# Decode attention kernel: TensorE's whole step sequence and most of VectorE's put into hardware loops

## The chip, the cores and the metric

One core of one Trainium2 chip runs the kernel. The metric is device microseconds of one execution (lower is better). Every number quoted as a time is a median over the kernel's runs; no slow run enters a comparison.

All instants below count from the span's start, that is, from the first instruction of the profiled execution. In the views of the profile PE is TensorE (PEld its weight loads), DVE is VectorE, ACT is ScalarE, POOL is GpSimd, and SPq is the queue of SyncE that issues the loads.

## The reference, cut to what matters

```python
B, Sq, D = 4, 1, 512
H, Sk, Dh = 32, 8192, 128
k_cache, v_cache: (B, H, Sk, Dh) bf16        # 268 MB each

q = (x_norm @ wq) -> (B, H, 1, Dh)
scores = einsum("bhqd,bhkd->bhqk", q, k_cache) * Dh ** -0.5
p = softmax(scores)
o = einsum("bhqk,bhkd->bhqd", p, v_cache)
h = x + o @ wo
out = h + glu(layernorm(h))                  # w_gate, w_up: 512x1792, w_down: 1792x512
```

One query per head against 8192 keys: 551 MB must be read, and every byte of K and V is used for one query row. Reading is the work.

## The kernel before

K and V are loaded in 64 tiles each (4 MB: two heads), K and V alternating, into a ring of four slots. A "step" is one head: VectorE transposes its K (four instructions of 1.2 us), TensorE makes the scores, and ten steps later TensorE multiplies the probabilities with V (PV). Eight steps make a group, whose softmax runs as a chain of small operations over all engines.

```python
GS = 8
LAG = 10
NS = 4
L0, LB = 16, 16          # steps 16..127 of TensorE are a loop of 7 turns of 16 steps

class _Prog:
    ...
    def emit(self, name, e):
        seen = {}
        turns = self.turns(name) if name == "pe" else []
        for op in self.ops[name]:
            if name == "pe" and op.turn is not None:
                if op is turns[0][0]:
                    self.emit_loop(name, e, turns, seen)
                continue
            ...                                  # any other operation: written out
```

```python
        # ring slots go round: wq, k0..k4, then k and v in turn
        for it in items:
            ...
            slot_of[it] = cur
            prev_of[it] = [owner[cur]] if owner[cur] is not None else []
            owner[cur] = it
            cur = (cur + 1) % NS
        ...
        def dve_T(s):
            it = ("k", s // 2)
            src, buf, base = slot_of[it], s % 2, (s % 2) * HT
            q = HT // 4
            op = None
            for i in range(4):
                def f(e, i=i):
                    return e.transpose(kT[:, buf, i * q:(i + 1) * q].bitcast(U32),
                                       ringv(src)[:, base + i * q:base + (i + 1) * q].bitcast(U32))
                op = P("dve", f, [dma_of[it][0], sc_of.get(s - 2)])
                yield
            T_of[s] = op
            consumed[it] = op
        ...
        for s in range(NST + LAG + 4):
            prog.turn = (s - L0) // LB if L0 <= s < NST else None
            ...                                  # the step's operations, with the groups' chains
```

A load of slot X waits until the tile that was in X has been consumed. Each engine's operations share one semaphore, so in the loop every turn must hold the same operations; small "blank" operations stood in for groups that do not exist yet. VectorE (661 instructions of work), ScalarE and the queue that issues the loads are written out in full.

## Time and profile before

| | before |
|---|---|
| time, median (6 runs) | 1289.76 us (1289.60 to 1290.04) |
| profiled span | 1288.0 us |
| data read | 550.77 MB at 428 GB/s |
| busy: TensorE, VectorE, ScalarE | 39%, 50%, 6% |

From the page of the kernel before: engines' busy time with share of the span, then two rows of 40 time slices (busy tenths of the DMA engines, GB/s), then the DMA queues (packets, MB, share of the 16 engines' span).

```profile
span 1288.0 us, 11045 instructions
PE 496.7 (39%) x4851; PEld 187.4 (15%) x4851; DVE 638.2 (50%) x661; ACT 77.3 (6%) x151; POOL 8.1 (1%) x23
...
DMA  9999999999999999999999999999999999999997
GB/s 407 431 430 431 431 430 432 429 432 428 436 431 431 431 432 433 430 434 430 434 429 435 430 433 429 434 429 435 428 436 427 436 427 436 428 435 429 434 429 311
...
q1 hardware_dynamic: 20384, 550.78, 99.5%
q8 instruction: 12, 0.20, 0.1%
q14 instruction: 7, 0.06, 0.0%
...
DMA 85%; PE 12%; DVE 2%; issue 0%; SPq 0%; DVEq 0%
```

What to read: the DMA engines are busy 90% or more in every slice but the last (70 to 80%), and the chain of work that ended last (the last line, by engine) is 85% DMA. No compute engine is full (50% at most). q8 and q14 are not data. The page calls their kind instruction and counts their packets, 12 and 7, on the same 16 DMA engines. They are 0.26 MB of 551 MB, 0.05%.

From the groups and the issue list of the kernel before (a group's last part is idle time of the engine before these instructions and what ended it; an issue's last number is us from issue to landing):

```profile
L457 DVE STREAM_TRANSPOSE kT<-ring 128x1024 uint32<-128x1024 uint32 x512 | 588.4, 1209 | 478.3 <-DMA ring<-in_A_k_cache_dram 478.3
...
ring<-in_A_k_cache_dram SPq DMA_DIRECT2D x64, 4096.0 KB, 29.7
ring<-in_A_v_cache_dram SPq DMA_DIRECT2D x64, 4096.0 KB, 33.8
...
kT<-in_A_wo_dram SPq DMA_DIRECT2D x1, 2560.0 KB, 40.4
```

VectorE waits 478 us for K tiles, so VectorE is not what holds the loads. A tile takes 9.71 us to stream, and 30 to 34 us pass from issue to landing, so two other tiles are queued ahead of each new one.

From the chain of work that ended last of the kernel before, two places (start us, us, what): each shown line is the first PV of every second V tile, so of every fourth tile in all, at the moment that tile had landed.

```profile
451.94 1.90 PE PS L504 x16
...
490.79 1.90 PE PS L504 x16
...
530.62 1.90 PE PS L504 x16
...
569.49 1.90 PE PS L504 x15
...
724.95 1.90 PE PS L504 x16
...
764.77 1.90 PE PS L504 x16
...
803.62 1.90 PE PS L504 x16
```

Four tiles take 38.85 us (490.79 - 451.94), as they should at 9.71 each. But 490.79 to 530.62 is 39.83, and 724.95 to 764.77 is 39.82: about once in 235 us the stream loses one microsecond.

The trace also records when each of a load's 16 increments of its semaphore arrives: every K and V tile shows 16 separate instants. I read each as one of the 16 DMA engines that the page counts, ending its share of the tile; the records do not name the engine. The work waits for the last of the 16: where TensorE had been idle for over 1 us before a PV (63 times), the PV started 0.04 us (median; 0.14 at most) after the last increment of a tile. I call the time from the first to the last of them the *lag* of the latest DMA engine. Worked out from these records (not a view of the profile), around one of the long intervals:

```
kernel before    last of 16 at   since last of tile before   first of 16, since first of tile before   lag
                 510.18 us         9.72                        9.73                                     2.30
                 520.86 us        10.68                        9.70                                     3.28
                 530.58 us         9.72                        9.71                                     3.29
```

The fastest DMA engine keeps its pace. One engine loses 0.98 us and does not get it back, and because the work on a tile starts after the last of its 16 increments, the whole kernel is 0.98 us later from there on. An 8 KB packet of q14 starts at 510.9 us.

### The profile page before, as it was taken

What the parts mean: (1) busy time and instruction counts of PE and PEld (TensorE: products, weight loads), DVE (VectorE), ACT (ScalarE), POOL (GpSimd) and SP (SyncE); (2) the same over time, 40 slices, a digit from 0 to 9 for tenths busy, and PEclk for the clock granted to TensorE, in tenths of its full rate; (3) what the DMA queues carried; (4) which work ended last, traced back from release to release, by engine and by line L of the source; (5) the groups of instructions that cost most, each with busy time, mean ns of one, the idle gap of its engine ahead of it and who ended that gap; (6) DMA issues with size and microseconds to landing.
All of it is one profiled execution on the core that took longest, in us unless ns stands there. A gap on an engine that the chain in (4) does not pass through costs nothing.

```text
span 1288.0 us, 11045 instructions
## 1 busy us (share of the span) xinstructions
PE 496.7 (39%) x4851; PEld 187.4 (15%) x4851; DVE 638.2 (50%) x661; ACT 77.3 (6%) x151; POOL 8.1 (1%) x23
## 2 busy tenths in 40 slices
PE   3434334335244244333334343252342442343445
PEld 1011111111011011111111111020110111111114
DVE  5974644535545545535536445455445446355300
ACT  2010100001010010100101000010100101000011
POOL 2000000000000000000000000000000000000000
PEclk9995565565665565665665665655655656655665
DMA  9999999999999999999999999999999999999997
GB/s 407 431 430 431 431 430 432 429 432 428 436 431 431 431 432 433 430 434 430 434 429 435 430 433 429 434 429 435 428 436 427 436 427 436 428 435 429 434 429 311
DMA packets 20411, 551.04 MB, mean 428 GB/s; under 512 B 2212, under 2 KB 2216, under 8 KB 3624
## 3 DMA queue, kind: packets, MB, share of 16 engines
q1 hardware_dynamic: 20384, 550.78, 99.5%
q8 instruction: 12, 0.20, 0.1%
q14 instruction: 7, 0.06, 0.0%
q10 hardware_dynamic: 8, 0.00, 0.0%
HBM read 550.77 MB, written 0.00 MB: 428 GB/s over the span
## 4 chain that ended last, share of the span: by engine, by line
DMA 85%; PE 12%; DVE 2%; issue 0%; SPq 0%; DVEq 0%
DMA ring<-in_A_v_cache_dram 79%; PE PS L504 7%; PE PS L482 4%; DMA ring<-in_B_w_up_dram 3%; DMA ring<-in_A_k_cache_dram 2%; DVE kT L457 1%; DMA ring<-in_A_wq_dram 1%; PE PS L535 0%; PE PS L387 0%; PE PS L720 0%; DVE Lq L430 0%; DVE ring L404 0%; PE PS L414 0%; PE PS L734 0%; DVE mx L518 0%
## 5 line engine op out<-in xcount | busy, mean ns | idle before, releaser
L457 DVE STREAM_TRANSPOSE kT<-ring 128x1024 uint32<-128x1024 uint32 x512 | 588.4, 1209 | 478.3 <-DMA ring<-in_A_k_cache_dram 478.3
L482 PE MATMUL PS<-kT,Lqg 128*32 128x512 bf16 x2048 | 241.7, 619 | 566.8 <-DVE kT L457 560.3
L504 PE MATMUL PS<-ring,PTz 128*32 128x512 bf16 x2048 | 215.1, 565 | 200.1 <-DMA ring<-in_A_v_cache_dram 200.1
L482 PEld LDWEIGHTS PS<-kT,Lqg 128*32 128x32 bf16 x2048 | 69.6, 135 | 697.2 <-DVE kT L457 449.4
L504 PEld LDWEIGHTS PS<-ring,PTz 128*32 128x32 bf16 x2048 | 65.8, 128 | 317.6 <-DMA ring<-in_A_v_cache_dram 190.1
L565 DVE STREAM_TRANSPOSE Et<-Ep 128x512 bf16<-128x512 bf16 x16 | 11.4, 711 | 96.3 <-ACT Ep L561 96.3
L539 ACT ACTIVATE negm<-PS 128x1 f32<-128x1 f32 x16 | 2.7, 171 | 672.3 <-PE PS L535 672.3
L574 ACT ACTIVATE PTz<-Et 64x512 bf16<-64x512 bf16 x32 | 34.0, 1061 | 12.8 <-DVE Et L565 12.5
L602 ACT ACTIVATE A_sb<-PS 32x32 bf16<-32x32 f32 x16 | 3.7, 231 | 480.3 <-PE PS L600 480.3
L579 DVE TENSOR_SCALAR Zs<-PS,rinv 128x512 f32<-128x512 f32 x16 | 11.6, 723 | 27.1 <-PE PS L504 27.1
L586 PE MATMUL PS<-SelZ,Zs 128*128 128x8 f32 x128 | 17.7, 265 | 0.9 <-DVE Zs L579 0.9
L586 PEld LDWEIGHTS PS<-SelZ,Zs 128*128 128x128 f32 x128 | 16.3, 199 | 10.2 <-issue 8.8
L518 DVE TENSOR_REDUCE mx<-PS 128x1 f32<-128x512 f32 x16 | 10.5, 657 | 4.3 <-PE PS L482 4.2
L541 ACT ACTIVATE E_sb<-PS,negm 128x512 bf16<-128x512 f32 x16 | 11.0, 687 | 0.5
L561 ACT ACTIVATE Ep<-PS 128x512 bf16<-128x512 f32 x16 | 9.6, 597 | 10.1 <-PE PS L557 10.1
L546 PEld LDWEIGHTS PS<-sig,Gsum 128*128 128x128 f32 x32 | 7.8, 304 | 13.1 <-issue 13.1
L546 PE MATMUL PS<-sig,Gsum 128*128 128x1 f32 x32 | 9.2, 356 | 0.0
L535 PEld LDWEIGHTS PS<-onesf,rowx 1*128 1x128 f32 x32 | 6.8, 262 | 12.3 <-issue 12.3
L535 PE MATMUL PS<-onesf,rowx 1*128 1x1 f32 x32 | 8.1, 321 | 0.0
L720 PE MATMUL PS<-hnT,ring 128*128 128x4 bf16 x112 | 7.0, 199 | 2.9 <-DMA ring<-in_B_w_gate_dram 2.1
L720 PEld LDWEIGHTS PS<-hnT,ring 128*128 128x128 bf16 x112 | 6.9, 161 | 3.1 <-DVE hnT L711 2.2
L557 PE MATMUL PS<-E_sb,Sel 128*32 128x512 bf16 x64 | 6.5, 400 | 1.9 <-ACT E_sb L541 1.1
(89 smaller groups left out, 93.2 us busy)
## 6 DMA issues: line engine op xcount, KB each, us to landing
ring<-in_A_k_cache_dram SPq DMA_DIRECT2D x64, 4096.0 KB, 29.7
ring<-in_A_v_cache_dram SPq DMA_DIRECT2D x64, 4096.0 KB, 33.8
ring<-in_A_wq_dram SPq DMA_DIRECT2D x1, 4096.0 KB, 12.3
kT<-in_A_wo_dram SPq DMA_DIRECT2D x1, 2560.0 KB, 40.4
ring<-in_B_w_gate_dram SPq DMA_DIRECT2D x1, 1792.0 KB, 39.7
ring<-in_B_w_up_dram SPq DMA_DIRECT2D x1, 1792.0 KB, 43.7
kT<-in_A_wo_dram SPq DMA_DIRECT2D x1, 1536.0 KB, 43.5
ring<-in_B_w_down_dram SPq DMA_DIRECT2D x1, 896.0 KB, 36.6
```

The lines of the kernel that those rows point to most:

```text
L457: return e.transpose(kT[:, buf, i * q:(i + 1) * q].bitcast(U32), ringv(src)[:, base + i * q:base + (i + 1) * q].bitcast(U32))
L482: mm = e.matmul(bS[g % 2][32 * j:32 * (j + 1), :], Lqg[:, g % 2, l0:l0 + 32], rhs, start=(s % GS == 0 and v == 0), stop=(s % GS == GS - 1 ...
L504: mm = e.matmul(bO[g % 2][32 * rq:32 * (rq + 1), :], PTz[:, g % 2, l0:l0 + 32], ringv(slot)[:, r0 * 128:(r0 + 4) * 128], start=(s % GS == ...
L518: mx_of[g] = P("dve", lambda e: e.tensor_reduce(mx[:, :], bS[g % 2][:, :], AX.X, ALU.max), [sc_of[g * GS + GS - 1], p1_of.get(g - 1)])
L535: p2_of[g] = P("pe", lambda e: e.matmul(bX[:, 0:1], rowx[0:1, :], onesf[0:1, 0:1], start=True, stop=True), [d2b_of[g], c_ones])
L541: exp_of[g] = P("act", lambda e: e.activation(E_sb[:, :], bS[g % 2][:, :], ACT.Exp, bias=negm[:, 0:1], scale=SCALE, accum_out=sig[:, 0:1]) ...
L546: L_of[g] = P("pe", lambda e: e.matmul(bX[:, 0:1], Gsum[:, :], sig[:, 0:1], start=True, stop=True), [exp_of[g], a1_of[g], d_g])
L565: et_of[g] = P("dve", lambda e: e.transpose(Et[:, :], Ep[:, :]), [epc_of[g]] + list(ptc_of.get(g - 1, ())))
L574: return e.activation(dst, src, ACT.Copy)
L579: z_of[g] = P("dve", lambda e: e.tensor_scalar(Zs[:, :], bO[g % 2][:, :], rinv[:, g % 2:g % 2 + 1], None, op0=ALU.mult), [pv_of[g * GS + G ...
L586: mm = e.matmul(bP[1][:, 0:8], Zs[:, 128 * r:128 * (r + 1)], SelZ[:, r, :], start=(r == 0), stop=(r == 3))
L720: mm = e.matmul(bk[:, B * t:B * t + B], wv[:, c, t:F:NFT], hnT[:, B * c:B * c + B], start=(c == 0), stop=(c == NDC - 1))
```

## The change

The intent is a smaller program: one loop body for each of TensorE (all steps, nine turns) and VectorE (all but the first 16 steps), in place of written-out steps. To allow it, each kind of operation gets its own semaphore, so a wait's value grows by a constant per turn even where groups are missing; missing groups are skipped by branches; a wait value that would be negative in turn 0 is held up; and the last V tiles keep alternating between two slots, so that the slot pattern is the same in every turn. The core of the diff:

```diff
-L0, LB = 16, 16
+LB = 16
...
+    def put(self, name, e, op, deps, seen):
+        for k, (v, s) in self.needs(name, deps).items():
+            if v > seen.get(k, 0):
+                e.wait_ge(s, v)
+                seen[k] = v
...
+    def emit(self, name, e):
+        seen = {}
+        t0 = self.loops.get(name)
+        done = False
+        for op in self.ops[name]:
+            if t0 is None or op.turn is None or op.turn < t0:
+                self.put(name, e, op, op.deps, seen)
+            elif not done:
+                done = True
+                self.emit_loop(name, e, t0, seen)
...
+        with e.Fori(t0, t1) as i:
+            n = 0
+            while n < len(body):
+                when = sorted(body[n])
+                ...
+                if len(when) == t1 - t0:
+                    guard = nullcontext()
+                elif when[0] == t0:
+                    guard = e.If(i < when[-1] + 1)
+                else:
+                    guard = e.If(i > when[0] - 1)
+                with guard:
+                    for ops in body[n:m]:
+                        self.emit_turns(name, e, ops, i, fixed, have)
...
+            e.wait_ge(vals[0][1][1], i * step + base if first >= 0 else i * step - smin(i, 1) * -base)
...
-    prog = _Prog()
+    prog = _Prog({"pe": 0, "dve": 1})
...
+            kind, t = it
+            if kind == "k":
+                cur = (1 + t) % NS if t < LAG2 else 2 * (t % 2)
+            elif kind == "v":
+                cur = 3 - 2 * (t % 2)
+            else:
+                cur = 2 if kind == "wd" else 0
             slot_of[it] = cur
             prev_of[it] = [owner[cur]] if owner[cur] is not None else []
             owner[cur] = it
-            cur = (cur + 1) % NS
...
-        def blank(s, base, eng):
...
-            prog.turn = (s - L0) // LB if L0 <= s < NST else None
+            prog.step = s
```

More of the change, by code (lines that the diff above doesn't have):

```diff
@@ L1 @@
-from contextlib import ExitStack
+from contextlib import ExitStack, nullcontext
 import concourse.bass as bass
 from concourse import mybir
+from concourse.expressions import smin
 BF16 = mybir.dt.bfloat16
@@ L17 @@
 NS = 4
-L0, LB = 16, 16
+LB = 16
 class _Op:
-    __slots__ = ("eng", "fn", "deps", "inc", "val", "sem", "turn")
+    __slots__ = ("eng", "fn", "deps", "inc", "val", "sem", "kind", "turn", "key")
     def __init__(self, eng, fn, deps):
@@ L37, with __init__, add, resolve @@
     ENGS = ("sp", "act", "dve", "pool", "pe")
-    def __init__(self):
+    def __init__(self, loops):
         self.ops = {e: [] for e in self.ENGS}
-        self.turn = None
-    def add(self, eng, fn, deps=(), sem=None, val=0):
+        self.loops = loops
+        self.step = None
+    def add(self, eng, fn, deps=(), sem=None, val=0, kind=None):
         op = _Op(eng, fn, deps)
-        op.sem, op.val = sem, val
-        op.turn = self.turn
+        op.sem, op.val, op.kind = sem, val, kind
+        op.turn = op.key = None
+        if self.step is not None:
+            op.turn, at = divmod(self.step, LB)
+            op.key = (at, kind, sum(o.kind == kind and o.turn == op.turn and o.key[0] == at
+                                    for o in self.ops[eng][-40:] if o.turn is not None))
         self.ops[eng].append(op)
         return op
-    def resolve(self, sems):
+    def resolve(self, sem_of):
         for e in self.ENGS:
@@ L55, in resolve, with needs @@
                         d.inc = True
-        self.step = {}
         for e in self.ENGS:
-            turns = self.turns(e)
-            for same in zip(*turns):
-                if any(op.inc for op in same):
-                    for op in same:
-                        op.inc = True
-            n = 0
-            for op in self.ops[e]:
-                if op.inc:
-                    n += 1
-                    op.sem, op.val = sems[e], n
-            if turns:
-                assert len({len(t) for t in turns}) == 1
-                self.step[id(sems[e])] = sum(op.inc for op in turns[0])
-    def turns(self, e):
-        by = {}
-        for op in self.ops[e]:
-            if op.turn is not None:
-                by.setdefault(op.turn, []).append(op)
-        return [by[k] for k in sorted(by)]
+            used = {op.kind for op in self.ops[e] if op.inc and op.kind is not None}
+            n = {}
+            for op in self.ops[e]:
+                if op.inc or op.kind in used:
+                    op.inc = True
+                    n[op.kind] = n.get(op.kind, 0) + 1
+                    op.sem, op.val = sem_of(e, op.kind), n[op.kind]
     @staticmethod
-    def needs(name, op, but=()):
+    def needs(name, deps):
         need = {}
-        for d in op.deps:
-            if d in but or d.eng == name == "pe":
+        for d in deps:
+            if d.eng == name == "pe":
                 continue
@@ L88, in needs @@
         return need
-    def emit(self, name, e):
-        seen = {}
-        turns = self.turns(name) if name == "pe" else []
-        for op in self.ops[name]:
-            if name == "pe" and op.turn is not None:
-                if op is turns[0][0]:
-                    self.emit_loop(name, e, turns, seen)
-                continue
-            for k, (v, s) in self.needs(name, op).items():
-                if v > seen.get(k, 0):
-                    e.wait_ge(s, v)
-                    seen[k] = v
+    def put(self, name, e, op, deps, seen):
[3 more added lines that the diff above has]
+                seen[k] = v
+        if op is not None:
             ins = op.fn(e)
@@ L104, in emit @@
                 ins.then_inc(op.sem, 1)
-    def emit_loop(self, name, e, turns, seen):
-        first = {}
-        fixed = [set(same[0].deps).intersection(*(op.deps for op in same[1:])) for same in zip(*turns)]
-        for op, ds in zip(turns[0], fixed):
-            for k, (v, s) in self.needs(name, op, set(op.deps) - ds).items():
-                if v > seen.get(k, 0):
-                    e.wait_ge(s, v)
-                    seen[k] = v
-        with e.Fori(0, len(turns)) as i:
-            for same, ds in zip(zip(*turns), fixed):
-                need = [self.needs(name, op, ds) for op in same]
-                for k in sorted({k for n in need for k in n}, key=lambda k: [k in n for n in need]):
-                    vals = [(t, n[k][0]) for t, n in enumerate(need) if k in n]
-                    s = next(n[k][1] for n in need if k in n)
-                    if k not in self.step:
-                        self.step[k] = (vals[-1][1] - vals[0][1]) // (vals[-1][0] - vals[0][0])
-                    base = {v - t * self.step[k] for t, v in vals}
-                    assert len(base) == 1, (vals, self.step[k])
-                    base = base.pop()
-                    if k in first and base <= first[k]:
-                        continue
-                    first[k] = base
-                    e.wait_ge(s, i * self.step[k] + base)
-                ins = same[0].fn(e)
-                if same[0].inc:
-                    ins.then_inc(same[0].sem, 1)
-        for k, base in first.items():
-            seen[k] = base + (len(turns) - 1) * self.step[k]
@@ new lines, in emit, with emit_loop, fixed @@
+    def emit(self, name, e):
[8 more added lines that the diff above has]
+                self.emit_loop(name, e, t0, seen)
+    def emit_loop(self, name, e, t0, seen):
+        turns = {}
+        for op in self.ops[name]:
+            if op.turn is not None and op.turn >= t0:
+                turns.setdefault(op.turn, {})[op.key] = op
+        t1 = max(turns) + 1
+        mid = (t0 + t1) // 2
+        body = []
+        for key in turns[mid]:
+            body.append({t: turns[t][key] for t in turns if key in turns[t]})
+        assert all(set(turns[t]) <= set(turns[mid]) for t in turns)
+        def fixed(d):
+            return d.turn is None and d.eng != "sp"
+        before = [d for ops in body for op in ops.values() for d in op.deps if fixed(d)]
+        self.put(name, e, None, before, seen)
+        have = {}
+        with e.Fori(t0, t1) as i:
+            n = 0
+            while n < len(body):
+                when = sorted(body[n])
+                m = n
+                while m < len(body) and sorted(body[m]) == when:
+                    m += 1
+                assert when == list(range(when[0], when[-1] + 1)) and (when[0] == t0 or when[-1] == t1 - 1)
+                if len(when) == t1 - t0:
[7 more added lines that the diff above has]
+                        self.emit_turns(name, e, ops, i, fixed, have)
+                n = m
+        for op in (op for ops in body for op in ops.values()):
+            for k, (v, s) in self.needs(name, op.deps).items():
+                seen[k] = max(seen.get(k, 0), v)
@@ new lines, in emit_turns @@
+    def emit_turns(self, name, e, ops, i, fixed, have):
+        need = {t: self.needs(name, [d for d in op.deps if not fixed(d)]) for t, op in ops.items()}
+        for k in dict.fromkeys(k for n in need.values() for k in n):
+            vals = [(t, n[k]) for t, n in sorted(need.items()) if k in n]
+            step = (vals[-1][1][0] - vals[0][1][0]) // (vals[-1][0] - vals[0][0])
+            base = {v - t * step for t, (v, s) in vals}
+            assert len(base) == 1, (vals, step)
+            base = base.pop()
+            if k in have and base <= have[k][0] and set(ops) <= have[k][1]:
+                continue
+            have[k] = (base, set(ops))
+            first = base + min(ops) * step
+            assert first >= 0 or (min(ops) == 0 and first + step >= 0)
+            e.wait_ge(vals[0][1][1], i * step + base if first >= 0 else i * step - smin(i, 1) * -base)
+        op = next(iter(ops.values()))
+        ins = op.fn(e)
+        if op.inc:
+            ins.then_inc(op.sem, 1)
@@ L195, in bass_sequential_preLN__mha_block_cached__glu_gated_glu__decode_kernel @@
         lnst = SB("lnst", [128, 16], FP32)
-        blk = SB("blk", [128, 4], FP32)
         xT = SB("xT", [128, NDC * B], FP32)
@@ L227, in bass_sequential_preLN__mha_block_cached__glu_gated_glu__decode_kernel, with sem_of @@
         bX, bH = bank[6], bank[7]
-        sems = {e: SEM("s_" + e) for e in _Prog.ENGS}
+        sems = {}
+        def sem_of(e, kind):
+            name = "s_" + (e if kind is None else kind)
+            if name not in sems:
+                sems[name] = SEM(name)
+            return sems[name]
         s_x = SEM("s_x")
@@ L253, in bass_sequential_preLN__mha_block_cached__glu_gated_glu__decode_kernel @@
         uses = [0] * NS
-        cur = 0
         for it in items:
@@ L458, in f @@
                                        ringv(src)[:, base + i * q:base + (i + 1) * q].bitcast(U32))
-                op = P("dve", f, [dma_of[it][0], sc_of.get(s - 2)])
+                op = P("dve", f, [dma_of[it][0], sc_of.get(s - 2)], kind="T" if i == 3 else "Tpart")
                 yield
@@ L468, in chain_lq @@
                 Lq[:, 64 * g:64 * g + 64].rearrange("p (i a) -> p i a", a=4), ACT.Copy),
-                [sc_of.get((g - 2) * GS + GS - 1), zlg] + ([o for ops in lq_of for o in ops] if g == 0 else []))
+                [sc_of.get((g - 2) * GS + GS - 1), zlg] + ([o for ops in lq_of for o in ops] if g == 0 else []), kind="lq")
         def pe_score(s):
@@ L490, in pe_score @@
                 deps += q_ev
-            sc_of[s] = P("pe", f, deps)
+            sc_of[s] = P("pe", f, deps, kind="sc")
         def pe_pv(s):
@@ L512, in pe_pv @@
                 deps.append(z_of.get(g - 2))
-            op = P("pe", f, deps)
+            op = P("pe", f, deps, kind="pv")
             pv_of[s] = op
@@ L518, in chain_mx @@
             mx_of[g] = P("dve", lambda e: e.tensor_reduce(mx[:, :], bS[g % 2][:, :], AX.X, ALU.max),
-                         [sc_of[g * GS + GS - 1], p1_of.get(g - 1)])
+                         [sc_of[g * GS + GS - 1], p1_of.get(g - 1)], kind="mx")
         p1_of, p2_of, a1_of, d2b_of = {}, {}, {}, {}
@@ L524, in chain_p1 @@
             p1_of[g] = P("pe", lambda e: e.transpose(bX[0:1, 0:128], mx[:, :], identf[:, :]),
-                         [mx_of[g], c_identf, d3_of.get(g - 1)] + ([o for ops in lq_of for o in ops] if g == 0 else []))
+                         [mx_of[g], c_identf, d3_of.get(g - 1)] + ([o for ops in lq_of for o in ops] if g == 0 else []), kind="p1")
         def chain_d2(g):
             d2_of[g] = P("dve", lambda e: e.tensor_reduce(
-                mrow[0:1, :], bX[0:1, 0:128].rearrange("p (j h a) -> p h j a", j=8, h=8), AX.XY, ALU.max), [p1_of[g]])
+                mrow[0:1, :], bX[0:1, 0:128].rearrange("p (j h a) -> p h j a", j=8, h=8), AX.XY, ALU.max), [p1_of[g]], kind="d2")
@@ L530, in chain_d2 @@
             d2b_of[g] = P("dve", lambda e: e.tensor_copy(
                 rowx[0:1, :].rearrange("p (j h a) -> p j h a", j=8, h=8),
-                bass.AP(mrow, 0, [[8, 1], [0, 8], [1, 8], [0, 2]])), [d2_of[g], p2_of.get(g - 1)])
+                bass.AP(mrow, 0, [[8, 1], [0, 8], [1, 8], [0, 2]])), [d2_of[g], p2_of.get(g - 1)], kind="d2b")
         def chain_p2(g):
             p2_of[g] = P("pe", lambda e: e.matmul(bX[:, 0:1], rowx[0:1, :], onesf[0:1, 0:1], start=True, stop=True),
-                         [d2b_of[g], c_ones])
+                         [d2b_of[g], c_ones], kind="p2")
@@ L538, in chain_exp @@
         def chain_exp(g):
             a1_of[g] = P("act", lambda e: e.activation(negm[:, :], bX[:, 0:1], ACT.Copy, scale=-SCALE),
-                         [p2_of[g], exp_of.get(g - 1)])
+                         [p2_of[g], exp_of.get(g - 1)], kind="a1")
             exp_of[g] = P("act", lambda e: e.activation(E_sb[:, :], bS[g % 2][:, :], ACT.Exp, bias=negm[:, 0:1],
                                                         scale=SCALE, accum_out=sig[:, 0:1]),
-                          [a1_of[g], sc_of[g * GS + GS - 1], mx_of[g], pt_of.get(g - 1), L_of.get(g - 1)])
+                          [a1_of[g], sc_of[g * GS + GS - 1], mx_of[g], pt_of.get(g - 1), L_of.get(g - 1)], kind="exp")
@@ L545, in chain_L @@
         def chain_L(g):
             L_of[g] = P("pe", lambda e: e.matmul(bX[:, 0:1], Gsum[:, :], sig[:, 0:1], start=True, stop=True),
-                        [exp_of[g], a1_of[g], d_g])
+                        [exp_of[g], a1_of[g], d_g], kind="L")
         def chain_d3(g):
-            d3_of[g] = P("dve", lambda e: e.reciprocal(rinv[:, g % 2:g % 2 + 1], bX[:, 0:1]), [L_of[g], z_of.get(g - 2)])
+            d3_of[g] = P("dve", lambda e: e.reciprocal(rinv[:, g % 2:g % 2 + 1], bX[:, 0:1]), [L_of[g], z_of.get(g - 2)], kind="d3")
@@ L559, in f @@
                 return mm
-            pt_of[g] = P("pe", f, [exp_of[g], c_sel, epc_of.get(g - 1)])
-            epc_of[g] = P("act", lambda e: e.activation(Ep[:, :], bP[0][:, :], ACT.Copy), [pt_of[g], et_of.get(g - 1)])
+            pt_of[g] = P("pe", f, [exp_of[g], c_sel, epc_of.get(g - 1)], kind="pt")
+            epc_of[g] = P("act", lambda e: e.activation(Ep[:, :], bP[0][:, :], ACT.Copy), [pt_of[g], et_of.get(g - 1)],
+                          kind="epc")
         def chain_et(g):
-            et_of[g] = P("dve", lambda e: e.transpose(Et[:, :], Ep[:, :]), [epc_of[g]] + list(ptc_of.get(g - 1, ())))
+            et_of[g] = P("dve", lambda e: e.transpose(Et[:, :], Ep[:, :]), [epc_of[g]] + list(ptc_of.get(g - 1, ())),
+                         kind="et")
             last_pv = [pv_of[(g - 2) * GS + GS - 1]] if g >= 2 else []
@@ L574, in fc @@
                     return e.activation(dst, src, ACT.Copy)
-                ops.append(P("act", fc, [et_of[g], zp] + last_pv))
+                ops.append(P("act", fc, [et_of[g], zp] + last_pv, kind="ptc"))
             ptc_of[g] = ops
@@ L579, in chain_z @@
             z_of[g] = P("dve", lambda e: e.tensor_scalar(Zs[:, :], bO[g % 2][:, :], rinv[:, g % 2:g % 2 + 1], None,
-                                                         op0=ALU.mult), [pv_of[g * GS + GS - 1], d3_of[g], ot_of.get(g - 1)])
+                                                         op0=ALU.mult), [pv_of[g * GS + GS - 1], d3_of[g], ot_of.get(g - 1)],
+                        kind="z")
         def chain_ot(g):
@@ L587, in f @@
                 return mm
-            ot_of[g] = P("pe", f, [z_of[g], d_selz, ac_of.get(g - 1)])
+            ot_of[g] = P("pe", f, [z_of[g], d_selz, ac_of.get(g - 1)], kind="ot")
         def chain_otc(g):
@@ L594, in chain_otc @@
                 bass.AP(PS, 5 * 512, [[4096, 128], [1, 8], [0, 4]]),
-                bass.AP(SelD, 0, [[4, 128], [0, 8], [1, 4]]), ALU.mult), [ot_of[g], d_seld, a_of.get(g - 1)])
+                bass.AP(SelD, 0, [[4, 128], [0, 8], [1, 4]]), ALU.mult), [ot_of[g], d_seld, a_of.get(g - 1)], kind="otc")
         def chain_a(g):
@@ L600, in chain_a @@
             a_of[g] = P("pe", lambda e: e.matmul(bP[1][0:32, 16:48], OD[:, :], SelS[:, :], start=True, stop=True,
-                                                 tile_position=(0, 0)), [otc_of[g], d_sels, ac_of.get(g - 1)])
+                                                 tile_position=(0, 0)), [otc_of[g], d_sels, ac_of.get(g - 1)], kind="a")
             ac_of[g] = P("act", lambda e: e.activation(A_sb[r0:r0 + 32, :, g // 4], bP[1][0:32, 16:48], ACT.Copy),
-                         [a_of[g]])
+                         [a_of[g]], kind="ac")
         def hook(s, base):
@@ L607, in hook @@
             return g if (s - base) % GS == 0 and 0 <= g < NG else None
-        def blank(s, base, eng):
-            if (s - base) % GS == 0 and L0 - GS <= s < L0:
-                def f(e):
-                    if eng == "act":
-                        return e.activation(blk[0:B, 0:1], lnst[0:B, 0:1], ACT.Copy)
-                    return e.tensor_copy(blk[0:B, base - 18:base - 17], lnst[0:B, 0:1])
-                P(eng, f, [d_a]).inc = True
         for s in range(NST + LAG + 4):
-            prog.turn = (s - L0) // LB if L0 <= s < NST else None
+            prog.step = s
             g = hook(s, 0)
@@ L643, in bass_sequential_preLN__mha_block_cached__glu_gated_glu__decode_kernel @@
                 chain_z(g)
-            else:
-                blank(s, 19, "dve")
             g = hook(s, 20)
@@ L648, in bass_sequential_preLN__mha_block_cached__glu_gated_glu__decode_kernel @@
                 chain_otc(g)
-            else:
-                blank(s, 20, "dve")
             if s < NST:
@@ L673, in bass_sequential_preLN__mha_block_cached__glu_gated_glu__decode_kernel @@
                 chain_a(g)
-            else:
-                blank(s, 20, "act")
-        prog.turn = None
+        prog.step = None
         gl = NG - 1
@@ L755, in bass_sequential_preLN__mha_block_cached__glu_gated_glu__decode_kernel @@
                 op.deps = [sc_of[NST - 1]] if it[0] == "wo" else [consumed[p] for p in prev_of[it]]
-        prog.resolve(sems)
+        prog.resolve(sem_of)
         with nc.Block() as block:
```

## The prediction

> **What bounds the kernel now.** The stream of loads. The page's DMA row is 9 in every slice, queue q1 takes 99.5% of the 16 engines' span, 550.77 MB arrive at 428 GB/s. The chain that ended last is 85% DMA. TensorE is busy 39%, VectorE 50%. From the landing records, a 4 MB tile lands every 9.71 us, all through the run. The issue list shows 29.7 us (K) and 33.8 us (V) from issue to landing, so about two tiles are queued ahead of each new one: an engine may free a slot some 20 us late before the queue runs dry.
>
> **What the change does.**
> 1. TensorE: steps 0-15 and the last PV-only steps enter the loop that already runs steps 16-127. Work is the same. Added are some 20-25 branches per turn. In the trace a register wait costs one ALU instruction of 32 ns and the loop's own branch 193 ns (mean of 7); 25 branches come to about 5 us of a 155 us turn (estimate), in an engine idle 60%. Off the path.
> 2. VectorE: steps 16 on become a loop. I estimate 170-250 instructions a turn (78 of work, some 50 register waits, some 10 guards): 8 turns at under 10 us of sequencer work each, most of it hidden under 1.2 us transposes; VectorE waited 478 us for K tiles (list of waits). Off the path.
> 3. Slots: the same until the last V tiles, which then alternate between two slots instead of four. In the timeline a V tile's PV ends about 4 us after landing and the next tile lands 9.7 us after it, so each load is still issued about 5 us before the queue would empty. No bubble, but lead time falls to about 15 us there.
> 4. Blank instructions: gone, nothing.
>
> **The one thing on the path: instruction fetch.** The landing records show that one of the 16 DMA engines ends each tile later than the rest: 2.0 us behind the fastest at 250 us, 5.3 us at the end. Its lag grows by about 0.98 us in the tiles where an 8 KB fetch of q14 (the instruction queue) falls, about 235 us apart, which is 128 VectorE instructions. The slowest engine sets the landing. With VectorE looping, three or four of these fetches vanish, and about three of the nine early 16 KB fetches of TensorE. The next slowest engine is 1.7 us behind, so at most 1.7 us is gained; ScalarE, still unrolled and with more separate semaphores to wait for, may fetch one block more and take some back. Gain: about 1 us.
>
> [...]no 16 KB fetch between 261 and 1225 us, though the body is about 70 KB. My VectorE body is 11-16 KB, so should stay.
>
> **Predicted time:** 1288.6 us, 8 in 10 between 1287.0 and 1291.5. Faster by over 2%: 0.01; within 2%: 0.95; slower by over 2%: 0.04.
>
> **What would show it.** DMA still 9 in all slices; tiles 9.71 us apart; q14 fetches fewer and the final lag between DMA engines nearer 4 than 5.3 us; no gap in the queue over the last five V tiles; waits of TensorE and VectorE shifted, not lengthened.
>
> **What would make it wrong.** VectorE's loop not staying in its buffer: two or three fetches a turn, on one DMA engine, 16 to 24 us (estimate) longer. Branches costing microseconds each, so that the last V tiles, with only about 5 us to spare, starve the queue.

The forecast's sum: at most 1.7 us, less what ScalarE's extra block takes, so about 1 us off 1289.76, put down as 1288.6 us. That VectorE's body should stay was the author's estimate; the trace of the kernel before shows only TensorE going round its loop with no fetch between 262 and 1226 us. The sizes of the two bodies are estimates from that trace too: 1132 instructions a turn of TensorE, and 170 to 250 of VectorE, at 64 bytes each (8192 bytes for the 128 instructions from one VectorE fetch to the next).

## The result

| | before | changed |
|---|---|---|
| time, median of 6 runs | 1289.76 us | 1286.87 us (1286.56 to 1287.01) |
| profiled span | 1288.0 us | 1285.0 us |
| TensorE instruction fetches (16 KB, q8) | 12 | 8 |
| other engines' instruction fetches in the span (8 KB and less, q14) | 7 | 5 |
| lag of the latest DMA engine at the last load | 5.16 us | 2.27 us |
| end of the last load on the fastest DMA engine | 1278.95 us | 1278.88 us |
| end of the last load on the latest DMA engine | 1284.11 us | 1281.15 us |

The ratio of the times is 0.9977 (95% interval 0.9964 to 0.9990). Ratios are the mean time of one kernel's fast runs over that of the other's of the same rounds, so not quite the ratio of the medians quoted. The gain is 2.9 us: small, but outside both kernels' scatter, and just outside the predicted range (1287.0 to 1291.5).

From the page of the changed kernel, the same parts:

```profile
span 1285.0 us, 11783 instructions
PE 499.6 (39%) x4851; PEld 187.0 (15%) x4851; DVE 634.8 (49%) x659; ACT 77.2 (6%) x150; POOL 8.3 (1%) x23
...
DMA  9999999999999999999999999999999999999998
...
q1 hardware_dynamic: 20384, 550.78, 99.7%
q8 instruction: 8, 0.13, 0.0%
q14 instruction: 5, 0.04, 0.0%
...
DMA 84%; PE 13%; DVE 2%; issue 0%; SPq 0%; DVEq 0%
```

More instructions are executed (11783 against 11045: branches and register arithmetic), the engines' work is the same, and less of the program is fetched. From the groups and issues of the changed kernel:

```profile
L497 DVE STREAM_TRANSPOSE kT<-ring 128x1024 uint32<-128x1024 uint32 x512 | 588.4, 1209 | 475.1 <-DMA ring<-in_A_k_cache_dram 474.9
...
ring<-in_A_k_cache_dram SPq DMA_DIRECT2D x64, 4096.0 KB, 29.5
ring<-in_A_v_cache_dram SPq DMA_DIRECT2D x64, 4096.0 KB, 33.6
...
kT<-in_A_wo_dram SPq DMA_DIRECT2D x1, 2560.0 KB, 21.4
```

VectorE's waits for K shrink by 3 us, the gain itself; they were not the cause. The lead of the output weights falls from 40.4 to 21.4 us because the last V tiles use two slots (22.0 us in the run with the new slots alone). From the chain of the changed kernel, the same two places:

```profile
451.66 1.90 PE PS L544 x16
...
490.52 1.90 PE PS L544 x15
...
529.37 1.90 PE PS L544 x16
...
568.23 1.90 PE PS L544 x16
...
723.68 1.90 PE PS L544 x14
...
762.54 1.90 PE PS L544 x12
...
801.39 1.90 PE PS L544 x16
```

Now 490.52 to 529.37 is 38.85 and 723.68 to 762.54 is 38.86. The lost microseconds are gone.

The landing records give a ledger: how the lag of one DMA engine behind the fastest moved in a tile in which an instruction fetch fell. The records do not name the engine of an increment; engines are told apart, from tile to tile, by their lag alone. Worked out from the records:

```
fetch at (us)                       kernel        one engine's lag moved from -> to
54.9, 278.0, 510.9, 746.3, 992.5    before, q14   0.38->1.35  1.38->2.35  2.30->3.28  3.39->4.35  4.36->5.29
54.5, 232.8                         changed, q14  0.15->1.12  1.15->2.13
22.2 ... 262.2 (eight, 16 KB)       before, q8    eight different engines, about 1.5 each (0.15->1.69, 0.10->1.62, ...)
1225.8, 1256.2                      before, q8    2.11->3.64  2.15->3.68
22.2 ... 125.2 (six, 16 KB)         changed, q8   six different engines, about 1.5 each
```

The five q14 fetches of the first row come 223 to 246 us apart and each starts where the one before had ended (within 0.1 us of drift): always the same DMA engine. They are VectorE's (the experiments below show it). In the changed kernel two of them are left.

### The profile page after: what moved, and what is told of

Read it like the earlier page. It is cut to its first block, busy times and chain, and to the rows that moved or that the text cites. A ratio compares the mean times of both kernels' runs of the same rounds, so it can differ in the third digit from the quotient of the medians.

```text
span 1285.0 us, 11783 instructions
## 1 busy us (share of the span) xinstructions
PE 499.6 (39%) x4851; PEld 187.0 (15%) x4851; DVE 634.8 (49%) x659; ACT 77.2 (6%) x150; POOL 8.3 (1%) x23
## 4 chain that ended last, share of the span: by engine, by line
DMA 84%; PE 13%; DVE 2%; issue 0%; SPq 0%; DVEq 0%
DMA ring<-in_A_v_cache_dram 79%; PE PS L544 8%; PE PS L522 4%; DMA ring<-in_B_w_up_dram 3%; DMA ring<-in_A_k_cache_dram 2%; DVE kT L497 1%; DMA ring<-in_A_wq_dram 1%; PE PS L575 1%; PE PS L427 0%; PE PS L748 0%; DVE Lq L470 0%; DVE ring L444 0%; PE PS L454 0%; PE PS L762 0%; SPq L325 0%
## 6 DMA issues: line engine op xcount, KB each, us to landing
kT<-in_A_wo_dram SPq DMA_DIRECT2D x1, 2560.0 KB, 21.4
```

## The experiments

The theory: the kernel ends when the most delayed DMA engine ends; an instruction fetch delays one DMA engine for good; the change is worth what it takes off the latest engine. Rivals: the gain is made by TensorE's own loop; it is made in the tail by the new slots; fetches are hidden and something else in the loops costs or saves time. All ten kernels gave correct results. They ran on several chips; the kernel before, timed beside each of them, stood between 1289.68 and 1289.88 us, so times may be compared across chips to a few tenths. The 95% intervals of the ratios are wider than that scatter, about 0.17% or 2.2 us to each side, so the argument rests on the ledgers and on the whole set of times, and not on any one ratio.

### VectorE written out again

```diff
-    prog = _Prog({"pe": 0, "dve": 1})
+    prog = _Prog({"pe": 0})
```

> The changed kernel with VectorE written out again and TensorE still in its loop. Theory (the load stream ends when its most delayed DMA engine ends, and each 8 KB fetch of VectorE's instructions costs that same engine 0.97 us): about five VectorE fetches come back, the lag of the last DMA engine returns from 2.4 to 5.0-5.4 us, and the time to 1289.4-1290.0 us, so the whole gain is gone. Rival 1 (the gain comes from TensorE's loop or its fewer 16 KB fetches) and rival 2 (from the new slots of the last tiles): the time stays at 1286.9 us.

Measured: 1290.88 us, beside 1289.76 us for the kernel before on the same chip (ratio 1.0010, interval 0.9994 to 1.0027). The whole gain is gone, and a little more. Six VectorE fetches fall in the stream instead of five, and one DMA engine's lag climbs in six steps of about 0.96 us to 5.93 us. The time is 0.9 us above the top of what I had expected. The sixth fetch, which I had not counted, goes with a longer program: with a semaphore per kind VectorE needs more wait instructions (805 records in all against 703). The lag explains 0.6 of the 1.1 us over the kernel before; about 0.5 us more is lost in one of the last tiles, where even the latest engine took 10.25 us (the tile that landed at 1233.09 us) and no fetch fell. That part stays unexplained. Rivals 1 and 2 fall: TensorE's loop and the new slots are both still in this kernel.

### TensorE written out entirely

```diff
-    prog = _Prog({"pe": 0, "dve": 1})
+    prog = _Prog({"dve": 1})
```

> The changed kernel with TensorE written out entirely and VectorE in its loop. Theory: about 38-40 fetches of 16 KB instead of 8, which so far each delayed a different DMA engine by 1.53 us, so two or three on each: the fastest engine ends about 3 us later than in the changed kernel, the slowest 2.4-4.6 us later, time 1289.3-1291.5 us. Rival (instruction fetches of TensorE are hidden; only VectorE's count): 1286.9 us.

Measured: 1293.03 us, 6.2 us over the changed kernel (ratio to before 1.0025, interval 1.0008 to 1.0041). From its DMA queues:

```profile
q8 instruction: 38, 0.62, 0.2%
q14 instruction: 6, 0.04, 0.0%
```

The direction was right and the size too small. The ledger shows why: the first eight fetches fall on eight different engines, the ninth (301 us) on one of them again (1.66->3.21), and after 16 fetches eight engines stand at 3.3 to 3.7 us. In this run they go round eight DMA engines, not sixteen, so 38 fetches come to four or five on each of the eight (an estimate, 38 / 8), and the latest is 8.0 us behind at 1205 us. Half of the engines are spared and the other half pay double; the latest of the slow half decides.

### The kernel before with the new slots only

```diff
             slot_of[it] = cur
             ...
-            cur = (cur + 1) % NS
+            (cur chosen per tile kind, as in the change)
```

> The kernel before with only the slot assignment of the changed one. Theory: no effect, 1289.8 us, within 0.3; the last engine's lag stays at 5.3 us. Rival 2 (the gain is made in the tail, where the output weights are now issued in one go after the last V tile): about 1286.9 us.

Measured: 1289.99 us beside 1289.76 us (ratio 1.0002, interval 0.9985 to 1.0018): no effect. The expected lag of 5.3 us was not quite met: it was 4.91 us before the last V tiles and then shrank to 2.5 us, yet the end did not move. I read it so: with two slots less is queued (the output weights land 22.0 us after issue instead of 40.4), and the fast DMA engines run out of work and wait for the latest (406 GB/s in the slice from 1191 to 1224 us, against 434 in the kernel before), while in this run the latest never waits (its tiles stay 9.7 to 9.9 us apart). Their lead was worth nothing.

### Four and eight fills a step, in the kernel before

One-byte fills on VectorE, written out, with nothing waiting for them; four a step add 512 instructions, eight 1024.

```diff
+                for j in range(1):              # range(2) for eight a step
+                    P("dve", lambda e, c=...: e.memset(pad[0:1, c:c + 1], 0))
                 yield
```

> The kernel before with four one-byte fills added to each of the 128 steps of VectorE, written out: 512 instructions, 32 KB, so four more 8 KB fetches. Theory: the last DMA engine's lag grows from 5.3 by 4 x 0.97 to about 9.2 us and the time to 1293.6 us (1292.6-1294.6). Rival (instructions of an engine that is half idle cost nothing): 1289.8 us.

Measured: 1293.31 us beside 1289.76 us (ratio 1.0028, interval 1.0011 to 1.0045), 3.55 us more.

> The kernel before with eight one-byte fills a step on VectorE, written out: twice the dose of the run with four, which cost 3.55 us. Theory: eight fetches of 8 KB more than in the kernel before, all on one DMA engine, lag at the end about 12.5-13 us, time 1296.5-1297.5 us. Rival (the four fills cost by something that saturates or by VectorE's busy time): clearly not in proportion; by busy time nothing, as VectorE stays idle a third of the span.

Measured: 1297.39 us beside 1289.88 us (ratio 1.0058, interval 1.0041 to 1.0075), 7.5 us more: in proportion. From the page of the kernel with eight fills:

```profile
PE 497.6 (38%) x4851; PEld 190.4 (15%) x4851; DVE 662.3 (51%) x1685; ACT 77.3 (6%) x151; POOL 8.3 (1%) x23
...
q8 instruction: 12, 0.20, 0.1%
q14 instruction: 15, 0.12, 0.0%
```

The fills cost VectorE 24 us of busy time (662.3 against 638.2), half idle as it was; that is not what is paid. q14 has eight packets more than before, and eight at 0.94 us (7.5 / 8) is the price. It also identifies the fetches of the first ledger row as VectorE's: 1024 instructions more make eight fetches more (15 against 7), so one fetch is 128 instructions, 64 bytes each (8192 / 128).

### Four, eight and twelve fills a step, inside VectorE's loop

```diff
+                for j in range(1):              # range(2), range(3)
+                    fill_of[s, i, j] = P("dve", lambda e, c=c: e.memset(pad[0:1, c:c + 1], 0),
+                                         [fill_of.get((s - LB, i, j))], kind=f"fill{i}{j}")
                 yield
```

> The changed kernel with the same four fills a step, now inside VectorE's loop (each also waits for its own write of the turn before, which adds a register instruction): VectorE executes over 900 instructions more, but the loop body grows to only about 250 instructions (16 KB). Theory: one or two fetches more than the two of the changed kernel, time 1287.0-1288.9 us. Rival (executed instructions cost, fetched or not): as in the unrolled kernel or more, 3.5 us over the changed kernel, 1290.4 us or later.

Measured: 1287.93 us (before on the same chip: 1289.88; ratio 0.9985, interval 0.9968 to 1.0001). VectorE executes 617 instructions more than in the changed kernel, more than the 512 that cost 3.55 us when written out, and pays 1.06 us, for one fetch more (three, the last engine going 0.48->1.43, 1.44->2.42, 2.43->3.39). So execution is not what costs. (I had counted a register instruction for every fill; most were not needed, so a turn has 204 instructions, 13 KB, and not 250.)

> The changed kernel with twelve fills a step in VectorE's loop: body about 500 instructions, 31-32 KB, [...]every turn fetches four or five blocks again, about 28-40 fetches of 8 KB on one DMA engine, 27-38 us more, time 1312-1326 us. If the whole body stays instead: three or four fetches more than the changed kernel, 1289-1291 us.

Measured: 1326.89 us (ratio to before 1.0283, interval 1.0266 to 1.0300). The one clear slowdown:

```profile
span 1325.4 us, 13424 instructions
...
DMA  9999999999999999999999999999999999999697
...
q1 hardware_dynamic: 20384, 550.78, 97.8%
q14 instruction: 43, 0.35, 0.1%
```

The body of 332 instructions a turn (21 KB, again less than I had counted; the next expectation, written with a miscount, says 318 and 20 KB) is no longer held: from 36 us on VectorE fetches 40 blocks, five in every full turn, on the one DMA engine. Why five, when the body is 2.6 blocks long, was not tested. 38 more than the changed kernel at 0.97 us are 36.9 us of the 40.0 measured. The rest comes in small pieces, most of it between 770 and 1100 us and about 0.7 us in the last tiles, and I did not trace it further. The 6 in the DMA row (1226 to 1259 us) falls where the lag drops from 17.0 to 5.4 us, that is, where the other engines wait longest. From about 670 us on the lag, 16 to 20.6 us, is about what two queued tiles can cover (19.4 us), and the other fifteen engines wait as well.

> The changed kernel with eight fills a step in VectorE's loop, between the four (204 instructions a turn, 13 KB, body kept, 1287.9 us) and the twelve (318 instructions, 20 KB, five fetches in each of eight turns, 1326.9 us): about 260 instructions a turn, 16-17 KB, three blocks of 8 KB. [...]the body stays, about five fetches in all, time 1288.5-1290.2 us. [...]four or five fetches in each turn again, 1318-1328 us.

(The outcomes, the body kept or fetched again in each turn, stand as alternatives.)

Measured: 1289.06 us (before: 1289.68; ratio 0.9993, interval 0.9976 to 1.0009). 268 instructions a turn (17 KB) are held: four VectorE fetches in all, the last at 253 us in the loop's first turn, lag 4.3 us. The limit lies between 17 and 21 KB of body for these positions in the program.

### Fills on ScalarE

```diff
+            for j in range(4 if s < NST else 0):
+                P("act", lambda e, c=4 * s + j: e.activation(pad[0:1, c:c + 1], lnst[0:1, 0:1], ACT.Copy), [d_a])
```

> The changed kernel with four one-element copies a step added on ScalarE, which is written out: 512 instructions, four more 8 KB fetches of another engine. Theory (each engine's 8 KB fetches always fall on one and the same DMA engine, as VectorE's do): ScalarE's DMA engine, about 1.7 us behind the fastest at the end, falls 2.6-4 us further behind and sets the end, time 1288.8-1290.3 us. If ScalarE's fetches go in turn over several DMA engines as TensorE's do: 1286.7-1287.6 us. Rival (VectorE is special, its own stall at the fetch is what costs): 1286.9 us.

Measured: 1288.97 us (before: 1289.68; ratio 0.9996, interval 0.9979 to 1.0013), 2.1 us over the changed kernel. Five ScalarE fetches after 250 us move one and the same DMA engine: 0.65->1.25->1.90->2.65->3.35->4.11 (small drift included). So VectorE is not special: the fetches of all three engines tested count, and those of ScalarE, too, stay on one DMA engine. ScalarE is busy 10% of the span here; its program still set the time of the kernel.

### TensorE's first 16 steps written out

```diff
-    prog = _Prog({"pe": 0, "dve": 1})
+    prog = _Prog({"pe": 1, "dve": 1})
```

> The changed kernel with TensorE's first 16 steps written out and the loop from step 16 (the rest of the change kept). The run with TensorE written out showed its 16 KB fetches go in turn over eight DMA engines, 1.55 us each. Theory: eight or nine such fetches in the stream instead of six, so at most one engine is hit twice: 1286.9 us with eight, up to 1288.2 us with nine or more. Rival (TensorE's early loop itself earned part of the gain): 1288 us or later even with eight fetches.

Measured: 1288.05 us (before: 1289.88; ratio 0.9986, interval 0.9969 to 1.0003), 1.2 us over the changed kernel. Eight 16 KB fetches fall before 300 us, on eight different engines, and until 1220 us the lag is 2.2 us, as in the changed kernel. Then the code after the loop is fetched, at 1268 us, while the last weights still stream, and being the ninth it lands on an engine that already had one: 1.94->3.49 us. So this part of the change is worth 1.2 us, through the ninth fetch (a tenth, at 1277 us, does much the same to another engine, 2.18->3.36), and the time alone would have fitted the rival as well; it was the ledger that told them apart.

### All runs in one table

"Lag" is that of the latest DMA engine at the last K or V tile landing before 1227 us; the difference is worked out.

| kernel | time, us | lag, us | time - lag |
|---|---|---|---|
| before | 1289.76 | 5.34 | 1284.4 |
| changed | 1286.87 | 2.38 | 1284.5 |
| VectorE written out | 1290.88 | 5.93 | 1285.0 |
| TensorE written out | 1293.03 | 8.02 | 1285.0 |
| before, new slots | 1289.99 | 4.91 | 1285.1 |
| before, 4 fills | 1293.31 | 8.62 | 1284.7 |
| before, 8 fills | 1297.39 | 12.82 | 1284.6 |
| changed, 4 fills | 1287.93 | 3.33 | 1284.6 |
| changed, 8 fills | 1289.06 | 4.34 | 1284.7 |
| changed, ScalarE fills | 1288.97 | 4.12 | 1284.9 |
| TensorE from step 16 | 1288.05 | 2.18 (3.42 at the last load) | 1285.9 (1284.6) |
| changed, 12 fills | 1326.89 | 17.15, engines waiting | no longer holds |

Over ten kernels and 10 us of time, the time is 1284.4 to 1285.1 us plus the lag of one DMA engine. The 0.7 us between them is not explained in full; in the kernels with VectorE or TensorE written out, some 0.5 us of it is lost even on the latest engine in the last V tiles. The changed kernel is the fastest; no experiment was made to find a faster one. What is left of its lag is one TensorE fetch (1.5 us) or two VectorE fetches on each of the late engines.

## Why the prediction was wrong

- **What bounds the kernel: right.** The stream of loads, set by its latest DMA engine. Time minus lag stays within 0.7 us over ten kernels.
- **TensorE's branches off the path: right.** 234 branches in nine turns are 26 a turn, as foreseen; they took 90 ns in the mean, 2.3 us a turn, hidden. VectorE's 72 took 47 ns in the mean.
- **VectorE's loop off the path and held: right**, with the body over-estimated: 125 instructions a turn (8 KB), not 170 to 250. Its last fetch came at 232.8 us, in the loop's first turn. TensorE, too, went round its loop of about 75 KB (an estimate: 1173 instructions a turn at the same 64 bytes) with no fetch between 125 and 1271 us.
- **Slots without effect: right** by the run with the slots alone (1289.99 against 1289.76 us).
- **Fetches that vanish: right.** Three of VectorE's five; two of TensorE's early eight (I had written three of nine); ScalarE fetched one block more, as I feared, on an engine that was not the latest. (The last early TensorE fetch starts at 262.2 us, not at 261.)
- **The failed step:** "The next slowest engine is 1.7 us behind, so at most 1.7 us is gained." The mechanism was right and this term of the sum was mis-sized: the room was 3.2 us, not 1.7. I read the second-latest lag at the end of the old run and took it as fixed. But two engines stood at 3.64 and 3.68 us there only because TensorE's two fetches at 1226 and 1256 us, for code after its loop, had just hit them a second time (from 2.11 and 2.15). The change removes those too (no TensorE fetch between 125 and 1271 us). Before them, at 1212 us, the second engine was 2.14 us behind the fastest and the latest 5.34 us: 3.2 us apart. Three vanished VectorE fetches at 0.97 us are 2.9 us, which fits into 3.2 but not into 1.7. The gain was 5.16 - 2.27 = 2.9 us of lag, and 2.9 us of time, while the fastest DMA engine ended at the same instant (1278.95 and 1278.88 us). "About 1 us" took something off even this for ScalarE's extra block, which cost nothing. That the two late fetches would have held the gain to 1.7 us is read from the ledger; no run kept them with VectorE in its loop. The nearest is the run with TensorE's first 16 steps written out, where one late fetch on an engine already hit cost 1.2 us. The prediction also took the engine that was 2.0 us late at 250 us for the one that was latest at the end: VectorE's engine stood at 1.38 us then and became the latest only with the fetch at 278 us.
- **What was not shown:** why an 8 KB fetch whose own packet takes 0.33 us (0.31 us for ScalarE's) costs its DMA engine 0.97 us (VectorE) or 0.6 to 0.7 us (ScalarE), and a 16 KB fetch of 1.0 to 1.1 us costs about 1.5 us. The prices are measured; the mechanism behind the excess stays open.

## What to carry to other kernels

In this kernel, bound by its loads (DMA engines busy 90% or more in 39 of 40 slices), the program itself was a load: the fetches of long, written-out code delayed the same DMA engines, and since the work on a tile started after the last of its 16 increments, the price was not the bytes (0.05%) but the sum of the fetches that fell on one engine (five of about 0.97 us before the change). In a kernel bound the same way, look at the spread of the 16 increments of one load at the start and the end of the run. If it grows in steps, try a shorter program for the engine whose fetches make the steps, even if that engine is idle most of the time (VectorE was busy 50% of the span here), and see that a loop body stays held (on VectorE 17 KB stayed, 21 KB was fetched again in every full turn). And when one late resource is relieved, do not take the next one's present position as the limit: ask which of its delays the same change takes away.
